# Hash attention and a three-way maxout feed-forward on one core: the fourth set's rows on SyncE, weights and values at units 52 to 57, the first batch in another order, third additions from unit 48

## The chip, the core and the metric

One core of a Trainium2 chip runs the whole program. Its engines are TensorE (PE in the profile, its weight loads PEld), VectorE (DVE), ScalarE (ACT), GpSimd (POOL) and SyncE (SP); each takes its own instructions in order, and they wait for each other by semaphores. The metric is the device time of one execution in microseconds (us).

## The reference

```python
q_bits = einsum('bhsd,dk->bhsk', q, proj) > 0          # 6 bits for each query, the same for k
mask   = q_bucket[..., :, None] == k_bucket[..., None, :]
scores = where(mask, q @ k.T / sqrt(64), -1e9)
attn   = softmax(scores)
x      = (attn @ v).transpose(0, 2, 1, 3).reshape(3072, 512)
out    = maximum(maximum(x @ w1, x @ w2), x @ w3) @ w_out
```

q, k and v are 4 batches x 8 heads x 768 positions x 64 in fp32, w1 to w3 are 512 x 768, w_out is 768 x 512, the output is 3072 x 512 in fp32.

## The kernel before

**Tiles.** A head's 768 positions are six blocks of 128. Queries are taken in two halves of 384. The hash is put into the score product: a tile `S` holds, for four heads, 64 rows of scaled values and below them rows of bits as +0.5 and -0.5, so that one matmul gives the score plus a term that is largest where all bits agree; after the exponential the others vanish. The exponentials go as fp16 into 26 buffers `AT`.

**Units.** The work is cut into 192 units of one head, one query half and one pair of key blocks. A unit is two score matmuls on PE (`scores`, L289) and one exponential on ACT (L291). Six units are a group (two heads, one query half); two groups of a query half make a quad of four heads. For a quad PE adds up the exponentials (`part_sums`, L366, into `sm`) and multiplies them with the values (`values`, L316, into `av`); DVE turns the sums into reciprocals (`inverse`, L325 to L327, L373) and scales (`scale`, L385) into `xT`, the input of the feed-forward part. A stretch of values and sums at one unit is called a burst; there is one at units 36, 48, 72 and then every 24 units. The first two quads of batch 0 are spread by `quad_at` (sums, first values, second values at three units each).

**Sums.** From unit 36 on `gather` (L341) adds the exponentials of a head's three units on DVE, so that the burst needs two sum matmuls for it; from unit 72 on a third addition (L343) puts the two halves together, and one is enough.

**Feed-forward.** `ffn_groups` makes 24 pieces for each of the eight halves of 384 tokens: 18 groups of four matmuls with w1, w2 or w3 (L404), whose PSUM results ACT copies (L411) or DVE takes the maximum with (L413), and six of three matmuls with w_out (L435). One piece goes with each unit, from unit 40 on.

**Set-up.** In batch 0 heads come in pairs (`pi` 0 to 3). `load_pair` brings their rows, `pair_turn` transposes them on PE, `pair_keep` copies PSUM to a tile `T32` (on DVE or ACT), `pair_place` (POOL, L143) scales them into `S`; `head_hash` and `first_bits` (pair 1) or `pair_hash` (pairs 2 and 3: PE L154, DVE L158) make the bits, which for pairs 2 and 3 go into `S` by four DMAs on SP each (L163). Pair 2 is used from unit 24, pair 3 from unit 30. From batch 1 on rows come in sets of four heads (`load_quad`, set `g` = 2 is the third, 3 the fourth; one half for k, side 1, and one for q, side 0): DVE transposes them (`turn`, L197, four for each half), POOL casts (`narrow`, L202), SP moves them into `S` (`place`, L208), PE hashes (`quad_hash`, L218), DVE makes the bits (L221) and SP sends them (L228). Set 2 is used from unit 48, set 3 from unit 60. `load_v` (L244, L248) and `load_weights` (L254, L258) are DMAs on POOL.

**What sets the order.** A list `at` is filled by `when(unit, function, ...)`, and the main loop emits for each unit: the scores one or two units ahead, what `at` holds for the unit, a piece of the feed-forward part, `gather`, the parts of `quad_at`, and a burst if one is due. Each engine executes its instructions in the order of this emission. Beside the data two things limit the order: score tiles and the other PSUM tiles (`ms`: transposes, hashes, sums, values, feed-forward groups) each go round in rings, and DMAs take turns on semaphores. The `ms` ring has four buffers until unit 10, two to unit 35, and three after that, when there are two for scores. DMAs of SP and ACT share eight semaphores in turn, and those of POOL have eight others: a DMA is issued only when the one eight places before it has landed.

Of the kernel before, what the change touches and what calls it, by code (L numbers as in the profile page):

```python
# [17 lines left out]
def kernel(  # L18
# [12 lines left out]
    nc = tc.nc  # L31
    B, H, S, D = q.shape
    NBITS = proj.shape[1]
    P = 128
# [100 lines left out]
    def pair_keep(pi, side, hd, mp, copy=nc.vector.tensor_copy):  # L135
        if pi not in t32:
            t32[pi] = t32_pool.tile([P, 2, S], FP32, tag="T32", name="T32")
        copy(t32[pi][:, side, hd * HALF : (hd + 1) * HALF], mp[:, 0:HALF])  # L138
# [38 lines left out]
    def first_bits(bp, side, hd, par, pi=0):  # L177
        j = 2 * side + par
        nc.vector.tensor_scalar(out=s_of[pi][D : D + NBITS, 2 * side + hd, par * HALF : (par + 1) * HALF],  # L179
                                in0=bp[Q * j : Q * j + NBITS, 0:HALF], scalar1=0.0, scalar2=0.5,  # L180
                                op0=AluOp.is_gt, op1=AluOp.subtract)
# [69 lines left out]
    def load_weights(i, c):  # L251
        if i == 3:
            n = NFB // 2
            nc.gpsimd.dma_start(wout_sb[:, c * n : (c + 1) * n, :],  # L254
                                moe_w_out.rearrange("(c p) f -> p c f", p=P)[:, c * n : (c + 1) * n, :])
            return
        src = (moe_w1, moe_w2, moe_w3)[i].rearrange("(c p w) f -> c p (w f)", p=P, w=D // Q)
        nc.gpsimd.dma_start(w_sb[i].rearrange("p (c w) f -> c p (w f)", w=D // Q)[c], src[c])  # L258


    groups = [(b, qh, jj) for b in range(B) for qh in range(2) for jj in range(HPAIR)]
# [13 lines left out]
    def place_of(g, hd, kp):  # L275
        if g < 4:
            return (g // 2) * 2 * UPG + hd * UPG + (g % 2) * MH + kp
        return g * UPG + hd * MH + kp
# [54 lines left out]
    def gather(u):  # L333
        g, hd, kp = unit_of(u)
        if u < 36 or kp == 0:
            return
        if kp == 1:
            as_of[g, hd] = as_pool.tile([P, 2, HALF], FP16, tag="as", name="As")
        t, new = as_of[g, hd], at_tiles[u % NAT][:, :, 0:HALF]
        old = at_tiles[(u - 1) % NAT][:, :, 0:HALF] if kp == 1 else t[:]  # L340
        nc.vector.tensor_tensor(out=t[:], in0=old, in1=new, op=AluOp.add)  # L341
        if kp == 2 and u >= 72:
            nc.vector.tensor_tensor(out=t[:, 0, :], in0=t[:, 0, :], in1=t[:, 1, :], op=AluOp.add)  # L343


# [1 line left out]
    def quads(gss):  # L347
        avs, rrs, rcs = {}, [], {}

        def part_values(i, w):  # L350
            avs[i, w] = values(gss[i], w, "ms" if i or w or "av" not in rings else "av")

        def part_sums():
            sm = ps_tile("sm")
            todo = []
            for i, gs in enumerate(gss):
                srcs = []
                for r in range(HQ):
                    g, hd = gs[r // 2], r % 2
                    t = as_of.pop((g, hd), None)  # L360
                    srcs.append([t[:, j, :] for j in range(1 if place_of(g, hd, 2) >= 72 else 2)] if t is not None else
                                [at_of(g, m, hd)[:, 0:HALF] for m in range(NM)])
                todo += [(i + len(gss) - 1, list(e)) for e in zip(*srcs)]
            for n, (i, e) in enumerate(todo):
                for r in range(HQ):
                    nc.tensor.matmul(sm[r * Q : (r + 1) * Q, 0:HALF], ones[:, i, :], e[r],  # L366
                                     start=(n == 0), stop=(n == len(todo) - 1))
            rrs.extend(inverse(sm, len(gss)))

        def scale(i, w):  # L370
            if i not in rcs:
                rcs[i] = rb_pool.tile([P, HALF], FP32, tag="rb", name="rb")
                nc.vector.transpose(rcs[i][:], rrs[i])  # L373
            gs, av, rc = gss[i], avs[i, w], rcs[i]
            sv = small.tile([P, 1], FP32, tag="sv", name="sv")
            nc.vector.tensor_scalar(out=sv[:], in0=av[:, HALF : HALF + 1], scalar1=EPS, scalar2=None, op0=AluOp.mult)
            (b, qh, jj), (b2, qh2, jj2) = groups[gs[0]], groups[gs[1]]
            c = 2 * (jj // 2) + w
            if jj2 == jj + 1:
                parts = [(0, P, xt_of(gs[0])[:, c, :])]  # L380
            else:
                o0 = jj % 2 * D
                parts = [(i * D, (i + 1) * D, xt_of(gs[i])[o0 : o0 + D, c, :]) for i in range(2)]
            for p0, p1, o in parts:
                nc.vector.scalar_tensor_tensor(out=o, in0=av[p0:p1, 0:HALF], scalar=sv[p0:p1, :], in1=rc[p0:p1, :],  # L385
                                               op0=AluOp.add, op1=AluOp.mult)

        return part_values, part_sums, scale


# [56 lines left out]
    def when(u, f, *args):  # L447
        at.setdefault(u, []).append(lambda: f(*args))

    with tc.manual_schedule():  # L450
# [26 lines left out]
        pair_turn(0, 1, 0, mk)  # L477
        pair_turn(0, 0, 0, mq)
        pair_keep(0, 1, 0, mk)
        pair_keep(0, 0, 0, mq, nc.vector.tensor_copy)  # L480
        first_hash(bk, 1, 0)
        first_hash(bq, 0, 0)
        mk1 = ps_tile("mp")
# [22 lines left out]
            t32.pop(0)  # L506

        when(0, first_rest)
        when(2, lambda: first_bits(rest[0], 0, 1, 1))

        def head_hash(pi, hd, last):
            bp = parts[pi, hd] = ps_tile("bp")
# [7 lines left out]
            first_bits(parts[pi, hd], side, hd, par, pi)  # L520

        parts = {}
        for pi, us, hs, offs, by_head, cs in ((1, (1, 2, 2, 3), (3, 6), (0, 0, 0, 0), 0, (1, 1, 0, 1)),):
            for u, c, (side, hd) in zip(us, cs, ((1, 0), (0, 0), (1, 1), (0, 1))):
                when(u, pair_group, pi, side, hd, nc.scalar.copy if c else nc.vector.tensor_copy)
                if hd == 1 or by_head:
                    for par in range(2):
                        when(u, pair_place, pi, side, par, *((hd, hd + 1) if by_head else ()))
            for hd in range(2):
                when(hs[hd], head_hash, pi, hd, hd == 1)  # L530
                for n in range(4):
                    when(hs[hd] + offs[n], head_bits, pi, hd, n)

        for pi, us, uh, cs in ((2, [4, 6, 9, 9], 12, [0, 1, 0, 0]), (3, [10, 13, 13, 16], 19, [0, 0, 0, 0]),):
            for u, c, (side, hd) in zip(us, cs, ((1, 0), (1, 1), (0, 0), (0, 1))):
                when(u, pair_group, pi, side, hd, nc.scalar.copy if c else nc.vector.tensor_copy)
                if hd == 1:
                    for par in range(2):
                        when(u, pair_place, pi, side, par)
            when(uh, pair_hash, pi)  # L540
        when(12, load_v, 1)
        for n, u in enumerate([2, 2, 12, 14, 16, 16, 28, 35]):
            when(u, load_weights, n // 2, n % 2)
        when(5, load_pair, 3, nc.sync)
        when(1, load_v, 0)
        for u, side, g, eng in ((1, 1, 2, nc.sync), (11, 0, 2, nc.sync), (22, 1, 3, nc.gpsimd), (28, 0, 3, nc.gpsimd)):
            when(u, load_quad, side, g, range(4), eng)
        hash_at = {}
        for g in range(2, NPAIR // 2):
            b2, i2 = divmod(g, 2)  # L550
            need = UPB * b2 + 12 * i2

            for n, side in enumerate((1, 0)):
                name = (side, g)
                if g < 4:
                    t0, dt = {2: (19, 18), 3: (33, 41)}[g][n], {2: 2, 3: 1}[g]
                else:
                    t0, dt = UPB * b2 - 47 + 24 * i2 + 12 * n, 3
                    for x in range(4):
                        when(t0 - 12 + x, load_quad, side, g, (x,), nc.gpsimd)  # L560
                for n2 in range(4):
                    when(t0 + dt * n2, turn, name, n2 // 2, n2 % 2)
                for u2 in range(2):
                    when(t0 + dt * (1 + 2 * u2) + 1, narrow, name, u2)
                when(t0 + (6 if dt == 1 else 4 * dt), place, name, range(4))
            hash_at[{2: 32, 3: 48}.get(g, UPB * b2 - 24 + 24 * i2)] = g
            when({2: 33, 3: 44}.get(g, need - 22), load_v, g)

        ffn = []
        ffn_at = {40: 0, 56: 1, **{24 * (h + 1) + 9: h for h in range(2, 2 * B - 1)}}  # L570
# [24 lines left out]
        def quad_at(gs, us, ua, ub):  # L595
            vals, sums, scale = quads([gs])
            for u, fs in ((us, [sums]), (ua, [lambda: vals(0, 0), lambda: scale(0, 0)]),
                          (ub, [lambda: vals(0, 1), lambda: scale(0, 1)])):
                firsts.setdefault(u, []).extend(fs)

        quad_at((0, 1), *[16, 19, 22])
        quad_at((2, 3), *[25, 29, 32])
        firsts.setdefault(32, []).append(lambda: hash_due(32))

        issued, MORE, LAST = 0, 11, 3 * UPB // 4
# [65 lines left out]
```

## Time and profile before

| | |
|---|---|
| three runs | 264.02, 262.35, 263.93 us, median 263.93 |
| profiled execution | 263.47 us, of which the span from the first to the last instruction is 261.4 |
| granted TensorE clock | 1.00 |
| PE busy | 253.0 us, 97% |
| DVE, ACT, POOL busy | 206.2, 181.5, 79.3 us |
| DMA | 30.92 MB, 118 GB/s over the span |

In the views that follow, a row of the timeline gives the start and length in us, the engine, line, operation, output and input, how many instructions it merges, and in brackets how long the engine stood idle before it and what ended that. An engine name with a q (SPq) is the queue that issues DMAs. Where a wait is for several things, the view names the one that came last by its reckoning.

### The profile page before, as it was taken

How to read it: one execution, taken by the hardware profiler on the slowest of the kernel's cores; microseconds unless marked ns; L12 is line 12 of the kernel's file. 1: busy time of each engine (PE TensorE's matmuls, PEld its weight loads, DVE VectorE, ACT ScalarE, POOL GpSimd, SP SyncE). 2: the span in 40 equal slices, each digit the busy share in tenths (PEclk: the TensorE clock that was granted, in tenths of full speed). 3: DMA queues.
4: the chain of work that ended last, by engine and by line, in shares of the span. 5: the costliest groups of instructions: out<-in, count | busy, mean ns of one | idle time of the engine just before them, and what ended most of it. 6: DMA issues, size and time to landing. Idle time of an engine off the chain costs nothing.

```text
span 261.4 us, 5905 instructions
## 1 busy us (share of the span) xinstructions
PE 253.0 (97%) x2215; PEld 139.9 (54%) x2215; DVE 206.2 (79%) x468; ACT 181.5 (69%) x274; POOL 79.3 (30%) x130
## 2 busy tenths in 40 slices
PE   8989998899999999999999999999999999999994
PEld 3445444455555555555555555555555555555552
DVE  2786998799867999799989999898767984875450
ACT  3989886847996299927996399928996589703322
POOL 3588693872325217241234316010000000000000
PEclk9999999999999999999999999999999999999999
DMA  6998979996084904951092904520020003000203
GB/s 211 369 265 131 212 192 246 208 241 147 3 220 130 211 3 107 253 162 41 1 264 58 232 7 96 145 68 14 13 109 3 0 3 120 3 0 29 96 0 120
DMA packets 20747, 30.92 MB, mean 118 GB/s; under 512 B 2960, under 2 KB 15088, under 8 KB 20720
## 3 DMA queue, kind: packets, MB, share of 16 engines
q0 software_dynamic: 8736, 14.16, 26.9%
q1 hardware_dynamic: 11696, 16.01, 19.4%
q8 instruction: 17, 0.28, 0.5%
q10 hardware_dynamic: 288, 0.39, 0.4%
q14 instruction: 10, 0.08, 0.1%
HBM read 25.17 MB, written 6.29 MB: 120 GB/s over the span
## 4 chain that ended last, share of the span: by engine, by line
PE 89%; DVE 4%; ACT 2%; DMA 2%; issue 1%; SPq 0%; ACTq 0%
PE l L404 35%; PE sc L289 22%; PE l L435 11%; PE av L316 11%; PE bp L218 3%; ACT AT L291 2%; DMA S<-bits 2%; PE mp L132 2%; PE bp L174 1%; DVE S L179 1%; PE sm L366 1%; PE wp L476 1%; DVE xT L385 1%; PE l L424 1%; PE sc L404 0%
## 5 line engine op out<-in xcount | busy, mean ns | idle before, releaser
L291 ACT ACTIVATE AT<-sc 128x768 f16<-128x768 f32 x192 | 152.5, 818 | 48.2 <-PE sc L289 42.0
L404 PE MATMUL l<-xT,w_sb 128*128 128x384 f16 x568 | 112.1, 325 | 0.9 <-DVE ht L413 0.9
L289 PE MATMUL sc<-S 72*128 72x384 bf16 (+1 forms) x384 | 91.4, 326 | 2.6 <-ACT AT L291 2.3
L404 PEld LDWEIGHTS <-w_sb 128*128 128x128 f16 x576 | 55.4, 97 | 40.4 <-issue 1.6
L413 DVE TENSOR_TENSOR ht<-ht,l 128x384 f16<-128x384 f16 x95 | 52.1, 549 | 22.0 <-PE l L404 20.0
L289 PEld LDWEIGHTS <-S 72*128 72x128 bf16 (+1 forms) x384 | 36.2, 98 | 36.3 <-issue 10.2
L202 POOL TENSOR_SCALAR T<-T 128x768 bf16<-128x768 f32 x24 | 22.7, 947 | 76.0 <-DVE T L197 46.2
L435 PE MATMUL l<-wout_sb,ht 128*128 128x512 f16 x138 | 36.0, 378 | 0.0
L341 DVE TENSOR_TENSOR As<-As,AT 128x768 f16<-128x768 f16 x52 | 33.0, 634 | 2.3 <-ACT AT L291 0.2
L316 PE MATMUL av<-AT,vo 128*32 128x385 f16 x744 | 34.2, 327 | 0.0
L341 DVE TENSOR_TENSOR As<-AT,AT 128x768 f16<-128x768 f16 x52 | 29.7, 571 | 5.5 <-ACT AT L291 5.5
L411 ACT CAST ht<-l 128x384 f16<-128x384 f32 x47 | 22.4, 477 | 10.4 <-DVE ht L413 7.4
L197 DVE STREAM_TRANSPOSE T<-nat 128x384 f32<-128x384 f32 x48 | 26.6, 566 | 1.8 <-DMA nat<-in_q_dram 1.7
L316 PEld LDWEIGHTS <-vo 128*32 128x32 f16 x768 | 19.7, 96 | 14.9 <-issue 6.0
L385 DVE SCALAR_TENSOR_TENSOR xT<-av,sv,rb 128x384 f16<-128x384 f32 (+1 forms) x35 | 21.6, 617 | 1.2
L435 PEld LDWEIGHTS <-ht 128*128 128x128 f16 x138 | 13.3, 97 | 12.5
L439 ACT COPY osb<-l 128x512 f32<-128x512 f32 x23 | 13.4, 582 | 6.5 <-PE l L435 6.5
L343 DVE TENSOR_TENSOR As<-As 128x384 f16<-128x384 f16 x40 | 14.3, 358 | 1.4
L248 POOL DMA_DIRECT2D vo<-in_v_dram x24 | 13.4, 575 | 3.9 <-DMA wout_sb<-in_moe_w_out_dram 3.7
L143 POOL TENSOR_SCALAR S<-T 64x768 bf16<-64x768 f32 (+1 forms) x17 | 12.4, 731 | 4.6 <-DVE T L138 2.3
L191 POOL DMA_DIRECT2D nat<-in_q_dram x20 | 11.1, 570 | 1.8 <-DMA nat<-in_k_dram 1.6
L191 POOL DMA_DIRECT2D nat<-in_k_dram x20 | 11.1, 566 | 0.9 <-DMA vo<-in_v_dram 0.6
(55 smaller groups left out, 114.1 us busy)
## 6 DMA issues: line engine op xcount, KB each, us to landing
out_dram<-osb SPq DMA_DIRECT2D x23, 256.0 KB
S<-T SPq DMA_DIRECT2D x48, 96.0 KB
nat<-in_k_dram POOLq DMA_DIRECT2D x20, 192.0 KB, 6.0
nat<-in_q_dram POOLq DMA_DIRECT2D x20, 192.0 KB, 5.6
w_sb<-in_moe_w_dram POOLq DMA_DIRECT2D x6, 384.0 KB, 6.4
vo<-in_v_dram POOLq DMA_DIRECT2D x24, 96.0 KB, 5.1
nat<-in_k_dram SPq DMA_DIRECT2D x6, 192.0 KB
nat<-in_k_dram SPq DMA_DIRECT2D x3, 384.0 KB
```

What stands on the lines that cost most here:

```text
L191: eng.dma_start(nat[side, g][:, cc * w : (cc + 1) * w], src[cc])
L197: nc.vector.transpose(t32[name][:, u, half * HALF : (half + 1) * HALF], i_)
L202: nc.gpsimd.tensor_scalar(out=t16[name][:, u, :], in0=t32[name][:, u, :], scalar1=RS, scalar2=1.0, op0=AluOp.mult, op1=AluOp.mult)
L289: nc.tensor.matmul(sc[:, j, 0:HALF], s_of[kn][0 : D + nb, kx, m * P : (m + 1) * P], s_of[qn][0 : D + nb, qx, qh * HALF : (qh + 1) * HALF], ...
L291: nc.scalar.activation(at_tiles[u % NAT][:, :, 0:HALF], sc[:, :, 0:HALF], ActFn.Exp, bias=-SCALE * 0.25 * nb, scale=SCALE)
L316: nc.tensor.matmul(av[r * Q : (r + 1) * Q, 0 : HALF + 1], vt[:, x, c + w : c + D : D // Q], at_of(g, m, hd)[:, 0 : HALF + 1], start=(m == ...
L341: nc.vector.tensor_tensor(out=t[:], in0=old, in1=new, op=AluOp.add)
L385: nc.vector.scalar_tensor_tensor(out=o, in0=av[p0:p1, 0:HALF], scalar=sv[p0:p1, :], in1=rc[p0:p1, :], op0=AluOp.add, op1=AluOp.mult)
L404: nc.tensor.matmul(ps[:, 0:HALF], w_sb[wi][:, jc, fb * P : (fb + 1) * P], xt[:, jc, :], start=(jc == 0), stop=(jc == NJC - 1))
L411: nc.scalar.copy(as_l(hts[fb]), l)
L413: nc.vector.tensor_tensor(out=as_l(hts[fb]), in0=as_l(hts[fb]), in1=l, op=AluOp.max)
L435: nc.tensor.matmul(ps[:, 0:DM], hts[fb][:, tb * P : (tb + 1) * P], wout_sb[:, fb, :], start=(fb == 0), stop=(fb == NFB - 1))
```

## The change

The rows of set 3 are issued by SP at units 21 (k) and 23 (q) instead of by POOL at 22 and 28. The two halves of w_out are loaded at unit 52 instead of 28 and 35, the values of sets 2 and 3 at units 53 and 57 instead of 33 and 44. The loads of w1 to w3 are each cut in two (one for each of the two rows of a partition) and begin at unit 5 instead of 2. The third addition is made from unit 48 on instead of 72. In the first batch one PSUM copy of pair 0 goes from DVE to ACT, the transposes, copies and hashes of pairs 1 to 3, the transposes of sets 2 and 3 and the parts of the first two quads move by up to two units (those of set 2's key half close up by up to four), and some copies change between DVE and ACT.

```diff
-        src = (moe_w1, moe_w2, moe_w3)[i].rearrange("(c p w) f -> c p (w f)", p=P, w=D // Q)
-        nc.gpsimd.dma_start(w_sb[i].rearrange("p (c w) f -> c p (w f)", w=D // Q)[c], src[c])
+        src = (moe_w1, moe_w2, moe_w3)[i].rearrange("(c p w) f -> c p w f", p=P, w=D // Q)
+        for w in range(D // Q):
+            nc.gpsimd.dma_start(w_sb[i][:, c * (D // Q) + w, :], src[c, :, w, :])
...
-        if kp == 2 and u >= 72:
+        if kp == 2 and u >= 48:
             nc.vector.tensor_tensor(out=t[:, 0, :], in0=t[:, 0, :], in1=t[:, 1, :], op=AluOp.add)
...
-                    srcs.append([t[:, j, :] for j in range(1 if place_of(g, hd, 2) >= 72 else 2)] if t is not None else
+                    srcs.append([t[:, j, :] for j in range(1 if place_of(g, hd, 2) >= 48 else 2)] if t is not None else
...
-        pair_keep(0, 0, 0, mq, nc.vector.tensor_copy)
+        pair_keep(0, 0, 0, mq, nc.scalar.copy)
...
-        when(2, lambda: first_bits(rest[0], 0, 1, 1))
+        when(1, lambda: first_bits(rest[0], 0, 1, 1))
...
-        for pi, us, hs, offs, by_head, cs in ((1, (1, 2, 2, 3), (3, 6), (0, 0, 0, 0), 0, (1, 1, 0, 1)),):
+        for pi, us, hs, offs, by_head, cs in ((1, (1, 1, 2, 4), (3, 6), (0, 0, 1, 1), 0, (1, 1, 0, 1)),):
...
-        for pi, us, uh, cs in ((2, [4, 6, 9, 9], 12, [0, 1, 0, 0]), (3, [10, 13, 13, 16], 19, [0, 0, 0, 0]),):
+        for pi, us, uh, cs in ((2, [5, 6, 9, 10], 13, [0, 0, 0, 1]), (3, [11, 13, 14, 16], 17, [0, 1, 0, 0]),):
...
-        for n, u in enumerate([2, 2, 12, 14, 16, 16, 28, 35]):
+        for n, u in enumerate([5, 7, 14, 16, 16, 18, 52, 52]):
             when(u, load_weights, n // 2, n % 2)
-        when(5, load_pair, 3, nc.sync)
+        when(7, load_pair, 3, nc.sync)
         when(1, load_v, 0)
-        for u, side, g, eng in ((1, 1, 2, nc.sync), (11, 0, 2, nc.sync), (22, 1, 3, nc.gpsimd), (28, 0, 3, nc.gpsimd)):
+        for u, side, g, eng in ((2, 1, 2, nc.sync), (11, 0, 2, nc.sync), (21, 1, 3, nc.sync), (23, 0, 3, nc.sync)):
...
-                    t0, dt = {2: (19, 18), 3: (33, 41)}[g][n], {2: 2, 3: 1}[g]
+                    t0, dt = {2: (18, 18), 3: (34, 43)}[g][n], {2: 1, 3: 1}[g]
...
-            when({2: 33, 3: 44}.get(g, need - 22), load_v, g)
+            when({2: 53, 3: 57}.get(g, need - 22), load_v, g)
...
-        quad_at((0, 1), *[16, 19, 22])
-        quad_at((2, 3), *[25, 29, 32])
+        quad_at((0, 1), *[18, 20, 23])
+        quad_at((2, 3), *[26, 29, 32])
```

## The prediction

> **What bounds the kernel now.** I read the page's busy shares and chain first, then busy time in stretches of 10 us, then every gap of TensorE (PE) in the timeline.
>
> ```profile
> span 261.4 us, 5905 instructions
> PE 253.0 (97%) x2215; PEld 139.9 (54%) x2215; DVE 206.2 (79%) x468; ACT 181.5 (69%) x274; POOL 79.3 (30%) x130
> PE 89%; DVE 4%; ACT 2%; DMA 2%; issue 1%; SPq 0%; ACTq 0%
> ```
>
> ```profile
> core 0: us, PE busy (x) PEld busy (x) DVE busy (x) ACT busy (x) POOL busy (x), PEclk, DMA share, GB/s
> 10.00:20.00 10.00, 8.82 (x65) 5.02 (x64) 8.50 (x16) 9.14 (x15) 7.31 (x11) 1.00 1.12 299
> 30.00:40.00 10.00, 9.44 (x125) 4.28 (x118) 9.28 (x20) 8.02 (x12) 9.04 (x15) 1.00 0.84 189
> 40.00:50.00 10.00, 9.14 (x107) 4.96 (x106) 7.55 (x17) 7.91 (x12) 5.79 (x9) 1.00 1.20 230
> 50.00:60.00 10.00, 9.14 (x104) 4.92 (x104) 9.55 (x22) 4.56 (x8) 7.16 (x12) 1.00 1.13 251
> 60.00:70.00 10.00, 10.00 (x62) 5.79 (x60) 9.04 (x20) 9.15 (x14) 1.43 (x2) 1.00 0.27 63
> ```
>
> PE carries 89% of the chain, and from 60 us on it is never idle at full clock. So the change can act in two ways: close gaps before 60 us, or take PE work away. In 10 to 20 us ScalarE (ACT) is the fullest, in 30 to 40 us VectorE (DVE) is, with PE close behind. The gaps that are left:
>
> ```profile
> 17.67 0.81 PE L289 MATMUL sc<-S 70*128 70x384 bf16 x4 [0.63 <-ACT AT L291]
> 28.85 0.48 PE L289 MATMUL sc<-S 70*128 70x384 bf16 x2 [0.17 <-DMA S<-bits]
> 33.92 0.81 PE L289 MATMUL sc<-S 70*128 70x384 bf16 x4 [0.56 <-ACT AT L291]
> 44.90 0.48 PE L289 MATMUL sc<-S 70*128 70x384 bf16 x2 [0.63 <-ACT AT L291]
> 45.60 0.48 PE L289 MATMUL sc<-S 70*128 70x384 bf16 x2 [0.22 <-ACT AT L291]
> 50.60 0.81 PE L404 MATMUL l<-xT,w_sb 128*128 128x384 f16 x4 [0.60 <-DVE ht L413]
> 51.99 0.81 PE L404 MATMUL l<-xT,w_sb 128*128 128x384 f16 x4 [0.26 <-DVE ht L413]
> ```
>
> A gap costs some 0.16 us more than is listed: a row of two score matmuls is drawn 0.48 us long and one of four 0.81, so each further matmul adds 0.165, while the last is drawn at its full 0.32. The seven together cost 3.07 + 7 x 0.16 = 4.2 us, 1.6% of the span. That is nearly all there is to win before 60 us.
>
> **The gaps at 50.60 and 51.99 (fourth set's rows).** The listed releaser is the maximum on DVE, but DVE itself stood still just before:
>
> ```profile
> 37.27 2.14 POOL L191 DMA_DIRECT2D nat<-in_q_dram  x4
> 49.53 0.58 DVE L197 STREAM_TRANSPOSE T<-nat 128x384 f32<-128x384 f32 x1 [1.65 <-DMA nat<-in_q_dram]
> ```
>
> The query rows of set 3 are issued by GpSimd (POOL) at 37.27 to 39.41, and the transpose that waits for them starts at 49.53, after 1.65 us of waiting, with the maxima queued behind it. With three PSUM buffers for the feed-forward groups, PE stops two groups later. The change issues both halves of set 3 on SyncE (SP) at units 21 and 23, behind the bit DMAs of pair 3, which end at 30.61 in the rows below: the query rows are on their way by about 34, before 37.27, and their transposes move from unit 41 to 43, two units later. The wait goes. What is late next? From 45.6 DVE gets one more transpose (0.49), since one of the four of the key side now stands behind the burst of unit 36, and loses the wait of 1.65: net 1.1 us less, so the maxima come on time. I take both gaps as closed: 0.60 + 0.26 + 2 x 0.16 = **-1.2 us**. The bounds are -1.2 and 0, if ACT or DVE took the gap's place; in 50 to 60 us ACT is busy for 4.56 of 10 us, so not ACT.
>
> **Third additions from unit 48.** Eight more additions on DVE, and half the matmuls in the sums of the burst of unit 72:
>
> ```profile
> 84.14 0.65 PE sm L366 x16
> L343 DVE TENSOR_TENSOR As<-As 128x384 f16<-128x384 f16 x40 | 14.3, 358 | 1.4
> 59.40:83.00 23.60, 23.60 (x146) 13.32 (x146) 19.34 (x40) 21.82 (x33) 7.07 (x11) 1.00 0.45 119
> 89.00:112.30 23.30, 23.30 (x141) 13.29 (x138) 21.03 (x46) 21.46 (x33) 8.34 (x12) 1.00 0.47 123
> ```
>
> The 16 sum matmuls become 8: **-0.33 us** of PE in a stretch where it never idles. DVE pays 8 x 0.358 = 2.86 us between about 59 and 83 us, where it is busy 19.34 of 23.60. That makes 22.2 of 23.6, or 94%; in the same 24 units of the next batch it has these additions already, is busy 21.03 of 23.30 (90%), and PE is full in both. So I cost the additions at nothing; the cover is 4.26 us of DVE idle time. If it were gone, each addition would hold a maximum, and through it a PSUM buffer, for up to 0.36 us.
>
> **First batch dealt out anew.** The two hashes of pairs 2 and 3 go from units 12 and 19 to 13 and 17, the eight transposes of the third set come two at a time at units 18 to 21 instead of one at a time to unit 25, the first quad's sums and values one or two units later; two PSUM copies change from DVE to ACT.
>
> ```profile
> 20.59 0.85 PE L154 MATMUL bp<-T,pj 128*32 128x384 f32 x8
> 22.10 8.51 SPq L163 DMA_DIRECT2D S<-bits  x8
> 23.11 5.61 DMA S<-bits
> 28.35 0.72 SPq L163 DMA_DIRECT2D S<-bits  x1
> 36.47 1.25 DVE L385 SCALAR_TENSOR_TENSOR xT<-av,sv,rb 64x384 f16<-64x384 f32 x2
> 37.87 1.50 PE L218 MATMUL bp<-T,pj 128*32 128x384 f32 x16
> ```
>
> The eight bit DMAs are pair 2's four, then pair 3's. The second of pair 2's took 5.61 us to land, at 28.72, and released unit 24. The second of pair 3's, issued at 28.35, would by the same 5.61 land at 33.96: that is the gap at 33.92, and not ACT, to which it is put down. With the hash two units earlier this gap (0.72) goes. But I book little for it. Behind it PE's hash of the third set (37.87) stands right after DVE's last scaling of the quad before, 36.47 + 1.25 = 37.72, whose PSUM buffer it takes. DVE is full there (9.28 of 10), and the change puts the same transposes, reciprocals and scalings on it in another order. Where that full row starts is set by PE's hash of pair 3, now at 26.08; two units earlier at this stage's pace of 0.7 us (ACT's, the fullest engine from 10 to 20) is near 25, and before the change DVE's row begins there too, with the first quad's sums. For pair 2 the hash is one unit later, some 0.7 us; ahead of it PE comes 0.4 us earlier, because unit 5 no longer stands behind the transposes of pair 1's last quarter, and a wait at unit 24 falls into the slack that DVE leaves PE. I take **0** for the whole stage, between -1.5 (the gaps at 17.67 and 33.92 closed, 0.79 + 0.72, and no new one) and +1 (unit 24 waits longer and DVE's row starts late). The copy of the first query half goes to ACT, which then places three quarters 0.4 us later; PE waits at that point for DVE's bits, so I count nothing.
>
> The two gaps at 44.90 and 45.60 stay: behind the burst of unit 36 PE has nothing else to do between two exponentials, and the order there is unchanged.
>
> **Weights and values moved.**
>
> ```profile
> 51.66 0.82 POOL L202 TENSOR_SCALAR T<-T 128x768 bf16<-128x768 f32 x1 [0.17 <-DVE T L197]
> 54.95 0.95 POOL L202 TENSOR_SCALAR T<-T 128x768 bf16<-128x768 f32 x1
> wout_sb<-in_moe_w_out_dram POOLq DMA_DIRECT2D x2, 384.0 KB, 8.2
> 39.40 1.67 POOL L248 DMA_DIRECT2D vo<-in_v_dram  x3
> L435 PE MATMUL l<-wout_sb,ht x18: 377/378/381, 68.5 to 73.8; 128*128 128x512 f16 x18
> 83.03 1.10 PE av L316 x24
> w_sb<-in_moe_w_dram POOLq DMA_DIRECT2D x6, 384.0 KB, 6.4
> 14.41 1.15 POOL L258 DMA_DIRECT2D w_sb<-in_moe_w_dram  x2
> ```
>
> On POOL the last weight now stands behind the two casts of set 3 (51.66 and 54.95 now; about 1 us earlier then) and three row DMAs of 0.55, so it is issued near 56 and 57, and with 8.2 us lands at 64 to 65. It is first needed at 68.5 - 1.2 = 67.3: 2 us of cover. The values of the second batch follow, and are needed in the burst that starts at 83.03: 10 us of cover. So both cost nothing. The six other weight DMAs become twelve of half the size: 6 x 0.57 = 3.4 us more on POOL (1.15 for two), against 8 issues that leave it for SP. They are needed behind the score row at 45.60; issued by about 31 and with 6.4 us to land they have 8 us of cover.
>
> **The sum**, against the profiled execution (span 261.4, time 263.47, so 2.07 around it; the median of the three runs, 263.93, is 0.2% above it): 263.47 - 1.2 - 0.33 + 0 = 261.94, rounded to **262.0 us**.
>
> **A rule against the change.** The bits and casts of the third set share SP's queue with the eight loads that are new on it:
>
> ```profile
> 35.52 5.74 SPq L208 DMA_DIRECT2D S<-T  x8
> 41.36 4.94 SPq L228 DMA_DIRECT2D S<-bits  x4
> 53.62 0.49 PE L289 MATMUL sc<-S 72*128 72x384 bf16 x2
> 54.59 0.49 PE L289 MATMUL sc<-S 72*128 72x384 bf16 x2
> ```
>
> Now the casts' DMAs go out from 35.52, the bits to 46.30, and unit 48 takes them at 53.62 without a wait (units follow each other at 0.97). With eight loads ahead, and each issue held until the DMA eight places before it has landed, the casts start no earlier than the loads land. [...]
>
> **The rivals.**
> [...] The eight loads are issued between 29 and 34, when the twelve weight DMAs are on the way too. At 10 us each, the span from 39.41 to 49.53 that the last of these rows needed, they land by 44, the bits go out by 49, and with the 5.61 us of a bit DMA unit 48 starts at 55 instead of 52.4: +2.6, so 264.6. It decides when the bits land after 53.9. Against it: half of the traffic of 40 to 50 us (1.20 of the engines' time) has moved away, and the loads start before the crowd. Chance 0.10.
> Rival 2, *the first batch gains as well* (faster). The gaps at 17.67 and 33.92 go and DVE's row starts a us earlier: -1.5 more, 260.5. For it: both releasers are moved ahead. Against it: DVE is full from 25 to 40. Chance 0.22.
> Rival 3, *the additions bind* in units 48 to 71: up to 2.86 back, less than the 1.4 us of idle time that is left, so 262.0 + 1.5 = 263.5. It decides if DVE leaves the burst of unit 48 later than it does now. Chance 0.06.
> Rival 4, *the change does not do what it says*: the rows come early, but DVE's full row holds PE at another group instead, and the 1.2 us do not appear: 263.1. Chance 0.10.
> The forecast keeps 0.52, with 261.2 to 262.8 as its own range.
>
> **How the numbers follow.** A measurement of this kernel can tell about 1%, 2.6 us. Faster by more: most of rival 2 and the low edge of the forecast, 0.26. Slower by more: only the far end of rivals 1 and 3, or two of them together, 0.07. The rest, 0.67. The range goes from 260.2 (rival 2 with some more) to 264.4 (rival 1 nearly whole).
>
> **What would show it.** Right: no wait of DVE for the rows of set 3, no gaps of PE at feed-forward groups before the burst of unit 48, the sums of the burst of unit 72 in 0.33 us, the two gaps behind the burst of unit 36 still there, and the third set's hash on PE within 0.4 us of 37.87. Wrong: a wait of PE for a DMA at unit 24 or 48, for the last weight near 67 us, or gaps in 60 to 83 us that end with a maximum on DVE.

## The result, and the profile after the change

The changed kernel takes 261.88 us (median of 20 runs, 260.94 to 263.09) against 263.03 us (20 runs, 261.83 to 265.21): a ratio of 0.9961, with a 95% interval of 0.9945 to 0.9978. The gain is small, and its interval excludes 1. The predicted time was 262.0 us. The profiled execution took 261.68 us against 263.47, so the trace shows 1.8 us less where the medians show 1.15; why the two differ is the more instructive half of what follows.

The page's span, its busy shares and its chain by engine:

```profile
span 259.9 us, 5896 instructions
PE 252.7 (97%) x2207; PEld 139.8 (54%) x2207; DVE 208.1 (80%) x474; ACT 181.8 (70%) x276; POOL 78.0 (30%) x128
PE 91%; DVE 6%; issue 1%; ACT 1%; DVEq 0%
```

PE has 8 matmuls less and carries 91% of the chain instead of 89%; the 2% that the chain gave to DMA before are gone. Every gap of PE in the timeline from 10 to 85 us:

```profile
12.16 0.83 PE L174 MATMUL bp<-T,pj 128*6 128x384 f32 x8 [0.40 <-DVE S L179]
17.28 0.88 PE L290 MATMUL sc<-S 70*128 70x384 bf16 x4 [0.58 <-ACT AT L292]
34.19 1.17 PE L317 MATMUL av<-AT,vo 128*32 128x385 f16 x24 [0.21 <-DVE xT L386]
44.69 0.48 PE L290 MATMUL sc<-S 70*128 70x384 bf16 x2 [0.96 <-ACT AT L292]
45.39 0.48 PE L290 MATMUL sc<-S 70*128 70x384 bf16 x2 [0.21 <-ACT AT L292]
```

The gaps at feed-forward groups (50.60 and 51.99 before) have no successor. The gap at unit 30 (33.92 before) is gone; a small one that ends with DVE's scaling stands there now. Of the pair behind the burst of unit 36, the first has grown from 0.63 to 0.96 us. The other steps, in the timelines of PE, SP and DVE, and in the groups:

```profile
37.37 1.46 PE L218 MATMUL bp<-T,pj 128*32 128x384 f32 x16
82.59 0.50 PE L367 MATMUL sm<-As,ones 128*32 128x384 f16 x8
...
28.91 1.81 SPq L191 DMA_DIRECT2D nat<-in_k_dram  x4
30.83 2.72 SPq L191 DMA_DIRECT2D nat<-in_q_dram  x4
35.05 8.63 SPq L208 DMA_DIRECT2D S<-T  x8
43.77 2.96 SPq L228 DMA_DIRECT2D S<-bits  x4
...
49.13 0.56 DVE L197 STREAM_TRANSPOSE T<-nat 128x384 f32<-128x384 f32 x1
```

```profile
L344 DVE TENSOR_TENSOR As<-As 128x384 f16<-128x384 f16 x48 | 17.2, 358 | 1.7
```

The issues of the last weight (least, median and longest time of one issue in ns, first and last start in us):

```profile
L254 POOL DMA_DIRECT2D wout_sb<-in_moe_w_out_dram x2: 763/770/777, 56.3 to 57.0; - x2
```

The query rows of set 3 are issued at 30.83 to 33.55, and the transpose of them at 49.13 waits for nothing. The last weight is issued at 56.3 and 57.0. The sums of the burst of unit 72 take 0.50 us; in the same view of the kernel before they are

```profile
83.96 0.82 PE L366 MATMUL sm<-As,ones 128*32 128x384 f16 x16
```

Where the time went is seen best when the starts of the score rows are set side by side. PE starts its first score row at 7.96 us of the span in the trace of the kernel before, at 7.99 in that of the changed kernel and at 7.5 to 8.5 in the others, so each start is taken against the start of unit 0 in its own trace. The table gives the advance over the kernel before in us (negative: later), worked out from the start of each unit's first score row; the kernels below are those of the experiments.

```
unit              24     30     39     40     45     48     51     75
changed kernel   +0.07  +0.79  +0.56  +0.24  +0.24  +1.41  +1.41  +1.72
rows_only         0.00  -0.59  -0.54  -0.53  -0.53  +0.64  +0.63  +0.63
adds_only        -0.10  +0.01  -0.04  -0.03  -0.03  +0.99  +0.99  +1.31
first_only       +0.07  +0.79  +0.62  +0.32  -1.35  -0.18  -0.18  -0.19
hash19           -0.07  +0.56  -0.24  -0.53  -0.53  +0.64  +0.64  +0.95
rows_back        +0.07  +0.78  +0.55  +0.26  -1.42  -0.24  -0.25  +0.07
mq_dve           +0.18  +0.90  +0.66  +0.67  +0.67  +1.84  +1.65  +1.96
fill36           +0.07  +0.79  +0.31  +1.10  +0.68  +1.85  +1.49  +1.81
fill3            +0.07  +0.78  +1.30  +0.89  +0.69  +1.86  +0.92  +1.24
```

For the changed kernel: 0.56 from the first batch up to unit 39, 0.32 of it lost again at unit 40, 1.17 from the two gaps between units 45 and 48, 0.31 from the sums in the burst of unit 72. From there to the end nothing changes.

### The profile page after: what moved, and what is told of

It is laid out like the page before. It is cut to its first block, busy times and chain, and to the rows that moved or that the text cites. A ratio compares the mean times of both kernels' runs of the same rounds, so it can differ in the third digit from the quotient of the medians.

```text
span 259.9 us, 5896 instructions
## 1 busy us (share of the span) xinstructions
PE 252.7 (97%) x2207; PEld 139.8 (54%) x2207; DVE 208.1 (80%) x474; ACT 181.8 (70%) x276; POOL 78.0 (30%) x128
## 4 chain that ended last, share of the span: by engine, by line
PE 91%; DVE 6%; issue 1%; ACT 1%; DVEq 0%
PE l L405 36%; PE sc L290 22%; PE l L436 12%; PE av L317 10%; PE bp L218 3%; PE mp L132 2%; DVE xT L386 2%; PE bp L174 1%; DVE T L197 1%; DVE S L179 1%; PE wp L477 1%; PE sm L367 1%; PE bp L154 1%; ACT AT L292 1%; DVE rb L374 1%
## 5 line engine op out<-in xcount | busy, mean ns | idle before, releaser
L344 DVE TENSOR_TENSOR As<-As 128x384 f16<-128x384 f16 x48 | 17.2, 358 | 1.7
L179 DVE TENSOR_SCALAR S<-bp 6x384 bf16<-6x384 f32 x16 | 8.9, 555 | 2.7 <-PE bp L174 2.5
L374 DVE STREAM_TRANSPOSE rb<-rr 128x384 f32<-128x384 f32 x16 | 9.1, 569 | 0.1
```

## The experiments

### Each part alone

**Rows of set 3 alone.**

```
-(22, 1, 3, nc.gpsimd), (28, 0, 3, nc.gpsimd)
+(21, 1, 3, nc.sync), (23, 0, 3, nc.sync)        # in the kernel before
```

> The kernel before with one part of the change alone: the rows of set 3 are issued by SyncE at units 21 and 23 instead of by GpSimd at 22 and 28; the transposes stay at units 33 and 41. Theory (the two gaps at feed-forward groups near 50.6 and 52.0 hang on these rows alone): DVE's wait of 1.65 us for the rows is gone, both gaps are closed, 1.2 us less, 261.8 us against 263.0 of the kernel before; the score rows of units 35 to 45 start where they did. Rival 1 (DVE's full row holds PE at another group): the wait is gone, the time is 263.0. Rival 2 (the loads stand in the way of set 2's casts and bits on SyncE's queue): unit 48 waits for a DMA, 264 or more.

Measured: 262.83 us, ratio 1.0007 (0.9977 to 1.0037). Its gap of PE at unit 30, and its transpose of the query rows:

```profile
35.00 0.81 PE L289 MATMUL sc<-S 70*128 70x384 bf16 x4 [1.15 <-DMA S<-bits]
...
48.83 0.56 DVE L197 STREAM_TRANSPOSE T<-nat 128x384 f32<-128x384 f32 x1
```

DVE's wait and both gaps near 50 are gone (1.17 in the table between units 45 and 48), as the theory says. But the gap at unit 30 is 1.15 instead of 0.56: the bit DMAs of pair 3, issued just ahead of the eight loads on the same queue, land later, and the table shows 0.59 lost there. (In the other kernels with GpSimd's rows and the hash of pair 3 at unit 19 this gap is 0.45 and 0.52, in one trace each.) None of the three cases had this one, and the 1.2 us that the theory expects are not in the time. Three of the 12 runs are at a clock of 0.987 to 0.994.

**Third additions alone.**

```
-        if kp == 2 and u >= 72:
+        if kp == 2 and u >= 48:                  # and the same bound in part_sums
```

> The kernel before with one part alone: the third additions from unit 48 on. Theory: the sums of the burst of unit 72 go from 16 matmuls to 8, 0.33 us less, and eight additions of 0.36 us on DVE lie in its idle time: 262.7 us against 263.0. Rival (DVE binds in units 48 to 71, as it still has the 1.65 us wait for the rows ahead of it): a gap of PE at a feed-forward group that ends with a maximum, 263.0 to 264.5.

Measured: 263.02 us, ratio 0.9998 (0.9977 to 1.0020). The trace has the 0.32 (units 51 to 75) and no gap behind the additions. It also shows something else. Its transpose of the query rows, and the sums:

```profile
48.73 0.58 DVE L197 STREAM_TRANSPOSE T<-nat 128x384 f32<-128x384 f32 x1 [0.36 <-issue]
...
83.17 0.50 PE L366 MATMUL sm<-As,ones 128*32 128x384 f16 x8
```

Nothing ahead of unit 48 differs from the kernel before, the rows are still GpSimd's, and yet DVE stands for 0.36 us instead of 1.65 and PE has no gap near 50. The view names no releaser for the 0.36, but the last of the four loads, issued at 39.1, took 9.5 us and landed at 48.65, 0.08 us ahead of the transpose; in the kernel before it was issued at 38.9, took 10.6 and landed at 49.45, also 0.08 ahead. So this wait is not the same in every execution: it depends on when the rows happen to land. Two of the 12 runs are at a clock of 0.987 and 0.993.

**First batch alone** (copies, hashes of pairs 2 and 3, transposes of set 2, quads and their loads as in the change; all else as before).

> The kernel before with the first batch dealt out anew alone (copies, hashes of pairs 2 and 3 at 13 and 17, set 2's transposes at units 18 to 21, quads, load of pair 3 at 7 and of set 2's keys at 2); rows of set 3, weights, values and additions as before. Theory (the 0.2 to 0.5 us by which the whole change is ahead at units 35 to 45 come from here, by the gap at unit 30 that goes and DVE's full row that begins earlier): the same advance at units 35 to 45, and 262.8 us (262.5 to 263.0). Rival 1 (they come from the loads and weights that GpSimd no longer issues there): no advance, 263.0. Rival 2 (with the rows still late the advance is lost at DVE's wait for them): advance at unit 45, none behind unit 50, 263.0.

Measured: 262.51 us, ratio 0.9990 (0.9968 to 1.0011). So none of these three parts alone moves the time clear of the noise; the fourth, the weights and values moved, was not run alone. Up to unit 39 the advance is that of the whole change (0.79 at unit 30, 0.62 at 39), so it comes from this part. Then 1.67 us are lost between units 40 and 45, without any gap of PE. Busy time by stretch, with the granted clock as the third column from the right:

```profile
core 0: us, PE busy (x) PEld busy (x) DVE busy (x) ACT busy (x) POOL busy (x), PEclk, DMA share, GB/s
44.00:46.00 2.00, 1.48 (x9) 0.78 (x9) 1.86 (x5) 2.00 (x4) 1.84 (x3) 0.99 1.28 177
46.00:48.00 2.00, 2.00 (x8) 0.99 (x7) 1.54 (x3) 1.58 (x3) 1.90 (x4) 0.50 1.45 167
48.00:50.00 2.00, 2.00 (x10) 1.03 (x9) 1.71 (x4) 0.81 (x1) 0.65 (x2) 0.66 1.35 180
50.00:52.00 2.00, 2.00 (x14) 1.19 (x13) 1.94 (x5) 1.87 (x3) 1.94 (x4) 1.00 1.10 280
```

The clock fell to a half from 46 to a little over 49 us. While PE was slow the rows arrived, so the gaps near 50 did not appear either. Four of the 12 runs have a clock of 0.991 or 0.992, this one among them. This is the clue to the medians, and it is followed below.

**The hash of pair 3 back at unit 19 in the changed kernel.**

```
-(3, [11, 13, 14, 16], 17, [0, 1, 0, 0])
+(3, [11, 13, 14, 16], 19, [0, 1, 0, 0])
```

> The changed kernel with the hash of pair 3 back at unit 19 (from 17). Theory (the gap at unit 30 was the landing of the second bit DMA of pair 3, and DVE's full row behind it gives most of it back): the gap before unit 30 is back with 0.4 to 0.9 us, the hash of set 2 on PE is at most 0.3 us later than in the changed kernel, and the time is 261.9 to 262.2 against 261.9. Rival (PE, not DVE, sets the pace from 25 to 38): the whole gap appears in the time, 262.6 or more.

Measured: 262.09 us, ratio 0.9984 (0.9957 to 1.0010). A gap that ends with a bit DMA is back, but at unit 33, the first of pair 3's second head, and not at unit 30:

```profile
35.93 0.81 PE L290 MATMUL sc<-S 70*128 70x384 bf16 x4 [0.69 <-DMA S<-bits]
```

In the table the loss is 0.23 at unit 30, 0.80 at unit 39 (+0.56 against -0.24) and 0.77 at the end (+1.72 against +0.95). The theory, that DVE's full row would give most of it back, falls for the trace: all of it stays. The third set's hash on PE comes 0.79 us later against unit 0, where the theory allowed 0.3, and DVE is busy for only 8.19 of the 10 us from 30 to 40. So the earlier hash belongs to the move of the rows, whose trace is 0.8 us behind without it. In the time, 262.09 us with two of 12 runs at 0.993, little of it shows; the changed kernel was not run beside this one.

### The half clock

The records of all runs give the granted clock of each. A stretch like that of the first batch alone (0.50 and 0.66 in the rows from 46 to 50 above, together some 3.4 us at half clock) is 1.7 us in 261, a mean of 0.993. Runs of the kernel before: none of 64 at 0.993 or below. Of the changed kernel: 6 of 20, with spans of 261.0 to 261.3, while its 14 other runs have 259.1 to 260.2. The experiments of this section bear on it.

**Rows back on GpSimd in the changed kernel** (units 22 and 28 again).

> The changed kernel with the rows of set 3 back on GpSimd at units 22 and 28, all else as changed. Theory (the early rows are worth the two gaps, 1.2 us, only in those executions in which GpSimd's rows land after 49; in others nothing): 261.9 to 263.0, mean some 0.6 above the changed kernel, with more spread of the spans at full clock (0.6 us against 0.3). Rival 1 (the rows are worth 1.2 in every run): 263.1. Rival 2 (the gain comes from the first batch and the additions alone): 261.9.

Measured: 263.75 us, ratio 0.9987 (0.9969 to 1.0005). Five of 6 runs at 0.991 to 0.992, the profiled one among them:

```profile
core 0: us, PE busy (x) PEld busy (x) DVE busy (x) ACT busy (x) POOL busy (x), PEclk, DMA share, GB/s
43.00:45.00 2.00, 0.84 (x5) 0.29 (x3) 1.86 (x7) 1.71 (x3) 0.00 (x0) 1.00 0.91 155
45.30:48.70 3.40, 3.40 (x13) 1.59 (x11) 2.91 (x6) 2.24 (x4) 3.20 (x5) 0.50 0.31 88
```

Half clock for 3.4 us, right behind the gaps of 0.94 and 0.22 us; in the 2 us from 43 to 45 PE was busy for 0.84. The one run at full clock has a span of 260.4. What early rows are worth on their own can't be read from these runs, since the clock covers it. The trace has one thing more. With weights and values out of GpSimd's queue the last load of the query rows, issued at 38.0, landed 8.0 us later, at 46.0, and DVE did not wait for it (it waited 1.76 us for key rows, at 40.87). So part of what the early rows do may come from the weights that moved; no run parts the two.

**The copy of the first query half back on DVE.**

```
-pair_keep(0, 0, 0, mq, nc.scalar.copy)
+pair_keep(0, 0, 0, mq, nc.vector.tensor_copy)
```

> The changed kernel with the copy of the first query half back on DVE, so that ACT has one instruction less from the start on. Theory (the exponential of unit 38 starts 0.36 us late in the changed kernel, and not in the kernel before, because of where it stands in ACT's instruction stream): the late start goes to another instruction and the gap at 44.7 is 0.63 as before the change; 261.5 in a run at full clock, and fewer runs at 0.992. Rival (the late start comes from what runs beside it): it stays at unit 38 with 0.36, 261.9.

Measured: 261.08 us, ratio 0.9895 (0.9877 to 0.9913); no run of 4 below full clock, spans 259.0 to 259.8. Its gaps of PE behind the burst of unit 36:

```profile
43.87 0.48 PE L290 MATMUL sc<-S 70*128 70x384 bf16 x2 [0.64 <-ACT AT L292]
44.57 0.48 PE L290 MATMUL sc<-S 70*128 70x384 bf16 x2 [0.22 <-ACT AT L292]
```

The start of ACT's exponentials there, in the timelines of the kernel before, of the changed kernel, and of this one:

```profile
44.03 2.96 ACT L291 ACTIVATE AT<-sc 128x768 f16<-128x768 f32 x4 [1.93 <-PE sc L289]
```

```profile
43.83 2.96 ACT L292 ACTIVATE AT<-sc 128x768 f16<-128x768 f32 x4 [2.25 <-PE sc L290]
```

```profile
43.01 2.96 ACT L292 ACTIVATE AT<-sc 128x768 f16<-128x768 f32 x4 [1.93 <-PE sc L290]
```

ACT stood 2.25 us in the changed kernel and 1.93 in the two others, so 0.32 of it is a late start after the scores were there: ACT starts 0.92 us behind the start of this score row on PE (42.91) in the changed kernel, and 0.59 and 0.60 behind it in the two others. With one instruction less ahead of it on ACT the late start is gone from unit 38, the first gap is 0.64 again, and the table has no loss at unit 40. That fits the theory, by which the place in ACT's instruction stream decides; what at that place costs 0.3 us no run settles. This kernel is ahead of the changed one by 0.24 us in the trace (1.96 against 1.72), and its interval against the kernel before lies below those of the changed kernel (0.9961 above, 0.9964 below), though the two were not run side by side, and beside this one (and beside the two with the score units that follow) the kernel before had spans of 261.4 to 262.8, mean 261.94, against a mean of 260.92 beside the parts alone. The ratios of different sets are therefore not to be compared to better than 0.4%.

**Two score units inside the burst of unit 36**, in the changed kernel and in the kernel before:

```
+                if u == 36 and n == ahead: fill(u + 2)    # scores of unit 38, behind the sums
                 vals(i, w)
+                if u == 36 and n == ahead: fill(u + 3)    # scores of unit 39
```

> The changed kernel, and in the burst of unit 36 the scores of units 38 and 39 are issued inside the burst (ahead of and behind the second values) instead of behind it. Theory 1 (the gaps at 44.7 and 45.4 cost 0.96 + 0.21 and twice 0.16, and come from PE having nothing between two exponentials): both are gone, 1.2 to 1.5 us less in a run at full clock. Theory 2 (those gaps are also what lets the granted clock fall to a half for 3.4 us, which 6 of 20 runs of the changed kernel show with 0.992 and none of the kernel before): no run at 0.992 or below, so that the median falls by up to 1.5 and the mean by some 0.4 more: 260.4 us. Rival 1 (DVE, which is busy for 8.9 of the 10 us from 40 to 50, takes the gap's place at the maxima from 45 on): 261.5 to 261.9. Rival 2 (the clock falls for another reason): as many runs at 0.992 as before.

Measured: 261.55 us, ratio 0.9906 (0.9889 to 0.9924); no run of 5 at 0.993 or below.

> The kernel before with the same two score units inside the burst of unit 36 and nothing else. Theory: its gaps at 44.9 and 45.6 (0.63 + 0.22 and twice 0.16) go, but PE then reaches the feed-forward groups near 50 a us earlier, while the rows of set 3 still land at 48.6 to 49.5, so that the wait for them takes the place: 262.0 to 263.0 against 263.05. Rival (the rows' wait is not what holds PE there): the whole 1.2 us, 261.9.

Measured: 264.18 us, ratio 1.0015 (0.9990 to 1.0040). The gap that is left in the changed kernel's version:

```profile
44.88 0.48 PE L290 MATMUL sc<-S 70*128 70x384 bf16 x2 [0.63 <-ACT AT L292]
```

Those near 50 in the other, and its busy time in one stretch, with the clock third from the right:

```profile
50.93 0.81 PE L404 MATMUL l<-xT,w_sb 128*128 128x384 f16 x4 [1.27 <-DVE ht L413]
52.32 1.14 PE L404 MATMUL l<-xT,w_sb 128*128 128x384 f16 x4 [0.26 <-DVE ht L413]
```

```profile
54.00:56.00 2.00, 2.00 (x8) 0.93 (x7) 1.90 (x5) 1.29 (x2) 1.91 (x4) 0.50 1.09 230
```

In the changed kernel one of the two gaps is closed, and no run has the half clock. Five runs alone would not show that: at 11 in 32, the share in all runs of the changed kernel, five in a row at full clock come by chance one time in eight. But with the copy on DVE there are four more, and beside these nine the rows back had five of 6 at half clock. In time only 0.44 us of the expected 1.2 is there at unit 45, and 0.36 is lost in the burst of unit 48 (1.85 to 1.49), as rival 1 has it. In the kernel before PE reaches the feed-forward groups earlier and waits longer for the late rows, 1.27 instead of 0.60; and in this trace the clock falls behind this gap, from 53 to 56 us, where in the traces of the first batch alone and of the rows back it is from 46 and from 45.3. The half clock follows the gap to its new place in this one trace.

**Three units inside the burst, with the copy on DVE; and the changed kernel beside it on the same chip.**

> The changed kernel once more, beside the next ones on one chip. Theory: the ratio is between 0.990 and 0.997; runs at full clock with spans near 259.9, about a third of the runs at 0.992 with spans 1.2 us longer, from the half clock behind the gaps at 44.7 and 45.4. Rival (the half clock is a matter of the chip alone): none at 0.992 here, or all.

Measured: 262.34 us, ratio 0.9964 (0.9943 to 0.9986); 5 of 12 runs at 0.992 or 0.993, with spans of 261.0 to 261.6 against 259.6 to 260.6.

> The changed kernel with the copy of the first query half back on DVE, and in the burst of unit 36 the scores of units 38, 39 and 40 issued ahead of the sums, behind them and behind the second values. Theory (each score unit then finds its PSUM buffer free, so that no gap is left at 44 to 46; before this the copy on DVE left 0.64 + 0.22 and twice 0.16, 1.2 us): 0.8 to 1.2 us less than with the copy alone, span 258.3 to 258.6, no run at 0.992. Rival (DVE, full from 44 to 54, holds PE at the maxima or at the burst of unit 48 instead): the same span as with the copy alone, 259.2, or only 0.1 to 0.4 less.

Measured: 261.80 us, ratio 0.9934 (0.9910 to 0.9958); none of 7 runs below full clock, spans 259.6 to 260.1. Its gaps behind unit 36, and its busy time from 44 to 54 us:

```profile
45.60 0.32 PE L405 MATMUL l<-xT,w_sb 128*128 128x384 f16 x1 [0.39 <-DVE xT L386]
53.41 0.81 PE L405 MATMUL l<-xT,w_sb 128*128 128x384 f16 x4 [0.31 <-DVE ht L414]
```

```profile
44.00:54.00 10.00, 9.29 (x56) 5.24 (x54) 9.83 (x21) 8.93 (x13) 5.14 (x8) 1.00 0.55 151
```

The two gaps are gone, PE is 1.30 us ahead at unit 39, and by unit 48 (+1.86 against +1.84 with the copy alone) nothing of it is left; at unit 51 it is 0.73 behind (+0.92 against +1.65). PE now waits for DVE's scaling and for its maxima, and DVE is busy 9.83 of 10 us. The rival had it right: behind these gaps stands a full DVE. With them closed none of 7 runs has the half clock, but with the copy alone none of four had it either, with spans of 259.0 to 259.8.

### How far the covers reach

**Last weight issued later** (units 56 and 57 instead of 52).

> The changed kernel with the two halves of the last weight issued at units 56 and 57 instead of 52. Theory (with 8.3 and 9.5 us to land, and needed at 67.2 and 68.1, the changed kernel has 2 us of cover): issued near 60.5 and 61.5, landing near 69 and 71, and a gap of PE of 1.5 to 3 us at the first group with the last weight; the time is that much longer, 263.3 to 265. Rival (the landing is shorter, because the engines carry less then): no gap, 261.9.

Measured: one run, 267.75 us, clock 0.985. Its gaps of PE at the last weight, and its busy time behind them:

```profile
69.36 0.81 PE L436 MATMUL l<-wout_sb,ht 128*128 128x512 f16 x3 [2.09 <-DMA wout_sb<-in_moe_w_out_dram]
71.45 1.44 PE L436 MATMUL l<-wout_sb,ht 128*128 128x512 f16 x3 [0.81 <-DMA wout_sb<-in_moe_w_out_dram]
```

```profile
70.00:75.00 5.00, 4.19 (x13) 1.55 (x12) 1.40 (x3) 2.21 (x3) 1.88 (x4) 0.52 1.16 292
```

A step of four units on paper became 7.7 us: GpSimd issued the halves at 64.0 and 64.8 instead of 56.3 and 57.0, behind a cast of its own. They landed 5.4 and 6.6 us after their issue, and PE stood 2.9 us. The time is 6 us longer, not 3: the clock fell to a half behind the first of the two gaps, from 70.2 to 77.1. So a cover of 2 us is thin, and in this run running out of it cost double.

**Rows of set 3 issued later on SyncE** (units 27 and 29).

> The changed kernel with the rows of set 3 issued on SyncE at units 27 and 29 instead of 21 and 23. Theory (SyncE's queue is in order, so casts and bits of set 2 stand behind the loads): the casts are issued some 4 us later, to 48, the bits to 50 or 51, and unit 48, which starts at 52.2, waits for a bit DMA by 1 to 4 us: 263 to 266. Rival (the casts' DMAs pass the loads, as they did not wait long before): no wait at unit 48, 261.9.

Measured: one run, 267.22 us, clock 0.987. Its longest gap of PE, SP's queue and DVE's wait, in the timeline:

```profile
48.79 0.48 PE L405 MATMUL l<-xT,w_sb 128*128 128x384 f16 x1 [2.75 <-DVE xT L386]
...
33.50 5.17 SPq L208 DMA_DIRECT2D S<-T  x8
38.77 2.76 SPq L191 DMA_DIRECT2D nat<-in_k_dram  x4
...
44.99 1.50 DVE L197 STREAM_TRANSPOSE T<-nat 128x384 f32<-128x384 f32 x3 [5.51 <-DMA nat<-in_k_dram]
```

Both cases missed. The loads went behind the casts (33.50, then 38.77), so the casts were not late at all. What was late was the key rows: DVE's transposes of them, due from unit 34 on, held its queue for 5.51 us, and with it the scalings of the burst of unit 36. Here too the clock fell to a half, from 46.8 to 53.7; the gap of 2.75 us lies from 46.04 to 48.79.

## Why the prediction came out, step by step

**The two gaps near 50: right in this trace, not in every run.** Booked -1.2, found 1.17, and the trace has no wait of DVE for the rows. But the step took one profiled execution for all. With GpSimd issuing the rows, one trace has 1.65 us of wait and two gaps, another 0.36 and none. The spans of the kernel before, all at full clock, go from 259.7 to 262.5 in 35 runs (mean 260.92), those of the changed kernel at full clock from 259.1 to 260.2 (mean 259.87). That the wider scatter is this wait was not tried by itself.

**The rows are not free where they are put.** The step costed the loads on SP at nothing beyond rival 1, by which set 2's casts and bits wait behind them on SP's queue. In the changed kernel that is so, but only because the hash of pair 3 is two units earlier; without it pair 3's bits land later, and 0.59 is lost at unit 30 in the one trace of the rows alone, 0.8 in that of the hash put back, behind a gap of 0.69 at unit 33. Rival 1 looked at another place: there casts wait behind the loads and unit 48 pays, here bits issued ahead of the loads came late and pair 3's units paid. That they were issued first did not keep them from it: the gap that ends with them is 1.15 us in the trace of the rows alone, against 0.56 at this place in the kernel before. What holds them up between issue and landing no run shows.

**Casts behind the loads: right.** They run from 35.05 to 43.68 instead of to 41.26 and the bits end at 46.73; unit 48 does not wait.

**Sums of the burst of unit 72: right**, 0.31 for 0.33. DVE is busy in the stretch as booked, and no gap appears between 60 and 83 us.

**First batch: 0 booked, 0.24 found**, inside the bounds. It is 0.56 up to unit 39, most of it the gap of the bits at unit 30, less 0.32 for a late start of ACT at unit 38. The gap at unit 30 was the landing of a bit DMA, as the step read it; the trace of the additions alone names this DMA for it. The reason for booking 0, that DVE's full row holds PE, is the weak part: the gap at 34.19 does end with DVE, but putting the hash back cost 0.8 us and none was given back. The step's own rows say as much, for from 30 to 40 us PE (9.44 of 10) is fuller than DVE (9.28), and not the other way round. The third set's hash came 0.50 us earlier, beyond the 0.4 that was named. So the 0 came near by two misses of opposite sign. The list of gaps also left out two ahead of 15 us (0.31 at 12.03 and 0.24 at 14.67), which no step uses.

**The two gaps behind the burst of unit 36: there, but not unchanged.** The order of PE's work is the same, as the step says; ACT's late start made the first 0.33 longer, and the prediction did not ask what two more instructions on ACT do downstream.

**Weights: right**, with 1.7 to 2.6 us of cover for the last one: its halves were in by 64.6 and 66.5, and the first groups with it start at 67.1 and 68.1.

**The sum.** 263.47 - 1.2 - 0.33 gives 261.94, and the medians are 261.88 and 262.34. That they lie so near is in part luck. The sum starts from one execution, which is 0.44 us above the median of the 20 runs (263.03), and books 1.53; the medians fell by 1.15 and 1.12, and the trace by 1.79. Beside the 0.24 of the first batch two things that the sum did not have lie in these numbers. The first is that the gain at full clock is smaller than the trace's, 1.33 us between the mean spans of the second comparison, where both kernels ran side by side (261.37 against 260.04); the wait that the kernel before does not have in all its runs would explain it. The second is the half clock, which costs 1.2 us in a third of the changed kernel's runs (11 of 32).

## What to carry to other kernels

A gap that ends with a DMA is a draw from a spread (the last load of the query rows took 10.6 us to land in the trace of the kernel before and 9.5 in that of the additions alone): before booking it whole, ask how the arrival scatters, and read several runs' spans. Closing one wait can move PE onto the next idle place (0.60 us near 50 became 1.27 in the kernel before with two score units in the burst), and there the price can double, when the clock falls as well: in the one run with the last weight later, 2.9 us of idle time became 6. Edits that look separable (a load on another queue, a hash two units earlier; here 0.8 us in the trace with the hash put back) should be costed together when they share a queue.

## What the runs showed of the hardware that was not expected

The granted clock of PE fell to a half for about 3.4 us behind some 1.2 to 1.5 us of idle time spread over two gaps: from 45.3 to 48.7 in the trace with the rows back, behind 0.94 and 0.22 listed, and from 46 to a little over 49 in that of the first batch alone, behind the same 0.94 and 0.22. In the kernel before with two score units in the burst it was as long, from 53 to 56, behind 1.27 and 0.26. With more idle time it was longer, in one run each: 6.9 us (70.2 to 77.1) with the last weight later, with 2.09 and 0.81 listed, and 6.9 (46.8 to 53.7) with the rows later, with 0.94, 0.22 and 2.75. The granted clock in the records of all runs shows how often: the kernel before, with 0.63 and 0.22 in its trace, has none of 64 runs at 0.993 or below; the changed kernel, with 0.94 to 0.96 and 0.21 to 0.22 in its two traces, has 11 of 32; with the rows back it was 5 of 6.

The length of these two gaps alone does not decide it. The changed kernel's two traces have them as long as the two traces that fell, and stay at full clock there. PE's busy time around the gaps in the first of the two, and ahead of the fall in the kernel before with two score units in the burst:

```profile
44.00:46.00 2.00, 1.09 (x6) 0.57 (x6) 1.97 (x5) 2.00 (x4) 1.16 (x2) 1.00 0.37 105
```

```profile
50.00:52.00 2.00, 1.07 (x6) 0.58 (x6) 2.00 (x5) 0.61 (x1) 1.09 (x3) 1.00 1.20 242
52.00:54.00 2.00, 1.74 (x8) 0.85 (x7) 2.00 (x5) 0.81 (x1) 1.94 (x3) 0.66 1.07 254
```

PE was busy for 1.09 of 2 us in the one and for 1.07 in the other; behind the first the clock stayed at 1.00 (46 to 50 us), behind the second it fell. What parts the runs that fall from those that do not was not shown. A few runs at 0.987 to 0.994 of the kernel before with one part changed (three of 12 with the rows alone, two of 12 with the additions alone) left no trace, and why they fell is open.

The second is ACT's late start: 0.3 us between scores that are ready and the exponential (0.92 us behind the start of the score row instead of 0.59 and 0.60), at one place of its stream, moved away by one instruction less. What causes it stays open.
